# A gated mix of two linear-attention branches on one core: x and two weights loaded by transposing DMAs in place of plain loads, TensorE transposes and copies

## The chip, the core and the metric

The kernel runs on one core of a Trainium2 chip. The core has five engines with a queue of instructions each: TensorE (PE; its weight loads are listed apart as PEld), VectorE (DVE), ScalarE (ACT), GpSimd (POOL) and SyncE (SP), which here only issues DMAs. ScalarE can issue DMAs too. All of them share 16 DMA engines. The metric is the device time of one execution in microseconds (us). The median of three runs of the kernel before is 398.64 us (396.17 to 399.18).

## What is computed

S = 2048 tokens of D = 640 bf16 numbers, 32 heads of 20. Two branches read the same x, and a gate mixes them. The first branch (A) is linear attention with softmax feature maps, the second (B) works in four segments of 512 tokens with causal softmax attention and a running memory.

```python
def _A_ref(x, wqkv, w_phi, wo):
    q, k, v = split(x @ wqkv)                      # per head, 20 wide
    pq = einsum('bhsd,hdf->bhsf', q, w_phi); pk = einsum('bhsd,hdf->bhsf', k, w_phi)
    phi_q = concat([softmax(pq), softmax(-pq)]); phi_k = concat([softmax(pk), softmax(-pk)])
    kv = einsum('bhsf,bhsd->bhfd', phi_k, v); z = einsum('bhsf->bhf', phi_k)
    o = einsum('bhqf,bhfd->bhqd', phi_q, kv) / (einsum('bhqf,bhf->bhq', phi_q, z)[..., None] + 1e-06)
    return merge_heads(o) @ wo
...
x = A_x
g = sigmoid((x * gate_w).sum(-1, keepdims=True))
return g * _A_ref(x, A_wqkv, A_w_phi, A_wo) + (1 - g) * _B_ref(x, B_wq, B_wk, B_wv, B_wo, B_beta)
```

## The kernel before, in words

Everything that contracts over D needs x with D on the partitions. So `xT` is [128, 5, 2048]: five blocks of 128 features, 2048 tokens each. In the kernel before, x comes in as eight plain loads of two chunks of 128 tokens (`x_nat`, `emit_xload`, L98 to L101, through a pool of six buffers), and `emit_xT` (L186) turns one chunk: five TensorE transposes into a PSUM tile `xtp` (L189), then one ScalarE copy to `xT` (L191).

The key projection of branch A and the feature map `w_phi` are both linear, so they are folded into one weight: `WkA` = Wk times a block-diagonal `Wphi`. The product needs Wk transposed. `emit_foldT` (L168) does that block row by block row: five transposes of `wnat_k` (L171) and a copy to `WkT` (L173). `emit_foldM` (L175) then multiplies `WkT` with `Wphi` in six pieces (L179) and copies the result to `WkA` (L184). `Wphi` is made on VectorE from `Wc` (the loaded `w_phi`) and a mask (L160). The query weight takes the same way into `WqA`, with `wnat_q` and the same `WkT` buffer, inside and after the main loop. `WvA` holds the value weight in two halves of 320 columns, with the gate weight `gw5` as column 320 of each (L312), so that the gate's logit comes out beside the values.

The order of the first stage is written out by hand for all engines (`manual_schedule`, L90): each engine's queue follows the program text. That stage is:

1. Loads. ScalarE's queue issues three of five pieces of `wnat_k`, SP the rest: `Wc`, two pieces of `wnat_k`, two `x_nat`, `gw5`, two halves of `WvA`, four more `x_nat`, `beta_b`, two more `x_nat`.
2. 25 transposes of the identity as a warm-up of TensorE (L299), the transposes of `wnat_k`, the five folds to `WkA`, and with them the first four chunks of `xT`.
3. The main loop over 16 chunks (L317). Each pass transposes chunk sc + 4, and `emit_a1` (L207) makes `pk` and `pv`, ten products each (L213), with `xT` as the stationary operand. Its column choice is strided: pass sc takes every fourth token of segment sc // 4, so the first four passes need the first 512 tokens. ScalarE makes exp(pk) and exp(-pk) in `Ek` (L217) and copies `pv` to `vA` (L219); VectorE sums `Ek` per head (`ksum`, L221) and takes the reciprocal (`krec`, L224); GpSimd multiplies them into `EkSn` (L225). `Ek` has three buffers, the PSUM pool `aps` four.
4. `emit_zmove` (L230), once per pass: two DMAs on SP's queue that lay the chunk of `EkSn` into `Z`, 16 destination partitions each, eight rows of 640 per partition. After the third pass SP also issues `wnat_q` (L323); passes 9 to 13 transpose it.
5. The five folds to `WqA`, then `kv_ps` = EkSn^T vA (L373) for five blocks j in the order 0, 3, 1, 2, 4, masked into `kvn` (L378). Between the blocks VectorE adds up the 32 rows of `Z` (`emit_zadd`, L238); the first of these additions needs all 32 Z moves, since each move fills every fourth row.
6. `pq` and its exponentials `Eq` (L266, L271), and from there the rest of branch A (L488 on) and branch B (L570 on).

SP works through its queue in order. Each DMA takes one of eight completion counters in turn, and an issue waits until the DMA that held the counter before has landed; so an issue can be held by one some eight places ahead of it, and it always follows what is queued before it.

Of the kernel before, what the change touches and what calls it, by code (L numbers as in the profile page):

```python
# [9 lines left out]
BF16 = mybir.dt.bfloat16  # L10
# [5 lines left out]
def kernel(  # L16
# [15 lines left out]
    nc = tc.nc  # L32
    P = 128
    S = 2048
    D = 640
    H = 32
    DH = 20
    KC = D // P
    NCH = S // P
    NSEG = 4  # L40
    L = S // NSEG
# [3 lines left out]
    x2 = A_x[0]  # L45
# [5 lines left out]
    xT = const.tile([P, KC, S], BF16, name="xT")  # L51
    beta_b = const.tile([P, H], BF16, name="beta_b")
    ident_b = const.tile([P, P], BF16, name="ident_b")
# [16 lines left out]
    Aw = a_stack.enter_context(tc.tile_pool(name="Aw", bufs=1, side="right"))  # L70
    wq_stack = ExitStack()
    wq_hold = wq_stack.enter_context(tc.tile_pool(name="wq_hold", bufs=1))
    x_stack = ExitStack()
    xload = x_stack.enter_context(tc.tile_pool(name="xload", bufs=6))
    aps_stack = ExitStack()
    aps = aps_stack.enter_context(tc.tile_pool(name="aps", bufs=4, space=bass.MemoryType.PSUM))

    wnat_k = wq_hold.tile([P, KC, D], BF16, name="wnat_k", tag="wnat")
    Wc = wq_hold.tile([P, KC, DH], BF16, name="Wc")
    x_nat = []  # L80
    WkA = Aw.tile([P, KC, D], BF16, name="WkA")
    WqA = Aw.tile([P, KC, D], BF16, name="WqA")
    WvA = Aw.tile([P, KC, 2, 321], BF16, name="WvA")
    xv = x2.rearrange("(c p) d -> p c d", p=P)

    def wsrc(lo):
        return A_wqkv[:, lo:lo + D].rearrange("(c p) n -> p c n", p=P)
# [3 lines left out]
        engines={mybir.EngineType.PE, mybir.EngineType.Activation, mybir.EngineType.DVE,  # L91
                 mybir.EngineType.Pool, mybir.EngineType.SP}))
    gw5 = const.tile([KC, P], BF16, name="gw5")
    for c in (0, 2, 4):
        nc.scalar.dma_start(out=wnat_k[:, c], in_=wsrc(D)[:, c])
    nc.sync.dma_start(out=Wc, in_=A_w_phi.rearrange("h f g -> (h f) g").rearrange("(c p) g -> p c g", p=P))

    def emit_xload():  # L98
        x_nat.append(xload.tile([P, 2, D], BF16, name="x_nat"))
        c0 = 2 * len(x_nat) - 2  # L100
        nc.sync.dma_start(out=x_nat[-1], in_=xv[:, c0:c0 + 2, :])  # L101

    for c in (1, 3):
        nc.sync.dma_start(out=wnat_k[:, c], in_=wsrc(D)[:, c])
    for n in range(2):
        emit_xload()
    nc.sync.dma_start(out=gw5, in_=gate_w.rearrange("(c p) -> c p", p=P))
    for bk in range(2):
        nc.sync.dma_start(out=WvA[:, :, bk, 0:320], in_=wsrc(2 * D)[:, :, bk * 320:(bk + 1) * 320])
    for n in range(4):  # L110
        emit_xload()
    nc.sync.dma_start(out=beta_b, in_=B_beta.partition_broadcast(P))

    nc.gpsimd.memset(ident_b, 0.0)
    nc.gpsimd.affine_select(out=ident_b, in_=ident_b, pattern=[[-1, P]],
# [42 lines left out]
    def emit_Wphi(j):  # L158
        h0, h1 = TH[j]
        nc.vector.tensor_tensor(out=Wphi[:, j, 0:h1 - h0, :],  # L160
                                in0=Wc[:, j:j + 1, :].to_broadcast([P, h1 - h0, DH]),
                                in1=wmask[:, j, h0:h1, None].to_broadcast([P, h1 - h0, DH]),
                                op=ALU.mult)

    def w2tile(name):
        return aps.tile([P, 2, 512], F32, name=name, tag="w2")

    def emit_foldT(wn, WT, ic, eng):  # L168
        tp = aps.tile([P, KC, P], BF16, name="wtp", tag="w2")
        for cc in range(KC):  # L170
            nc.tensor.transpose(out=tp[:, cc, :], in_=wn[:, ic, cc * P:(cc + 1) * P],  # L171
                                identity=ident_b)
        eng(out=WT[:, :, ic * P:(ic + 1) * P], in_=tp)  # L173

    def emit_foldM(WT, dst, ic):  # L175
        ps = w2tile("fold_ps")
        for n, (j, bk, lo, hi) in enumerate(PIECES):
            h0 = TH[j][0]
            nc.tensor.matmul(ps[:, bk, (lo - 16 * bk) * DH:(hi - 16 * bk) * DH],  # L179
                             lhsT=WT[:, j, ic * P:(ic + 1) * P],  # L180
                             rhs=Wphi[:, j, lo - h0:hi - h0, :].rearrange("p h d -> p (h d)"),
                             start=(n in FIRST), stop=(n in LAST))
        eng = nc.vector.tensor_copy if ic % 2 == 0 else nc.scalar.copy
        eng(out=dst[:, ic, :].rearrange("p (b n) -> p b n", b=2), in_=ps[:, :, 0:320])  # L184

    def emit_xT(sc):  # L186
        tp = aps.tile([P, KC, P], BF16, name="xtp", tag="w2")
        for c in range(KC):
            nc.tensor.transpose(out=tp[:, c, :], in_=x_nat[sc // 2][:, sc % 2, c * P:(c + 1) * P],  # L189
                                identity=ident_b)  # L190
        nc.scalar.copy(out=xT[:, :, sc * P:(sc + 1) * P], in_=tp)  # L191

    WkT = wq_hold.tile([P, KC, D], BF16, name="WkT")

    kv_stack = ExitStack()
    a1w = kv_stack.enter_context(tc.tile_pool(name="a1work", bufs=3, side="right"))
# [10 lines left out]
    def emit_a1(sc):  # L207
        pk, pv = w2tile("pk"), w2tile("pv")
        for ps, W, n in ((pk, WkA, 320), (pv, WvA, 321)):
            for bk in range(2):  # L210
                for c in range(KC):
                    rhs = WvA[:, c, bk, :] if W is WvA else WkA[:, c, bk * 320:(bk + 1) * 320]
                    nc.tensor.matmul(ps[:, bk, 0:n], lhsT=xTk[:, c, sc // 4, sc % 4], rhs=rhs,  # L213
                                     start=(c == 0), stop=(c == KC - 1))
        Ek = a1w.tile([P, 2, D], BF16, name="Ek")
        for sgn in range(2):
            nc.scalar.activation(out=Ek[:, sgn, :].rearrange("p (b n) -> p b n", b=2),  # L217
                                 in_=pk[:, :, 0:320], func=ACT.Exp, scale=1.0 - 2.0 * sgn)
        nc.scalar.copy(out=vA[:, sc], in_=pv[:, :, 0:321])  # L219
        ksum = a1w.tile([P, 2 * H], F32, name="ksum")  # L220
        nc.vector.tensor_reduce(out=ksum, in_=Ek.rearrange("p s (h f) -> p (s h) f", f=DH),  # L221
                                axis=AX.X, op=ALU.add)
        krec = a1w.tile([P, 2 * H], F32, name="krec")
        nc.vector.reciprocal(out=krec, in_=ksum)  # L224
        nc.gpsimd.tensor_tensor(  # L225
            out=EkSn[:, sc].rearrange("p s (h f) -> p (s h) f", f=DH),
            in0=Ek.rearrange("p s (h f) -> p (s h) f", f=DH),
            in1=krec[:, :, None].to_broadcast([P, 2 * H, DH]), op=ALU.mult)

    def emit_zmove(sc):  # L230
        g, r = divmod(sc, 4)
        for sgn in range(2):
            nc.sync.dma_start(out=Z[64 * sgn + 16 * g:64 * sgn + 16 * g + 16, r:32:4],
                              in_=EkSn[:, sc, sgn, :])
# [62 lines left out]
    warm = aps.tile([P, KC, P], BF16, name="warm", tag="w2")  # L297
    for n in range(25):
        nc.tensor.transpose(out=warm[:, n % KC, :], in_=ident_b, identity=ident_b)  # L299
    for n in range(KC):  # L300
        emit_foldT(wnat_k, WkT, n, nc.vector.tensor_copy if n in (0, 2) else nc.scalar.copy)
        if n == 3:
            for j in range(KC):
                emit_Wphi(j)
    for n in range(KC):
        emit_foldM(WkT, WkA, n)
        if n in (1, 3):
            for sc in (n - 1, n):
                emit_xT(sc)
    gw_ps = aps.tile([P, KC], BF16, name="gw_ps", tag="w2")  # L310
    nc.tensor.transpose(out=gw_ps, in_=gw5, identity=ident_b[0:KC, 0:KC])
    nc.vector.tensor_copy(out=WvA[:, :, :, 320:321],  # L312
                          in_=gw_ps[:, :, None, None].to_broadcast([P, KC, 2, 1]))
    for n in range(2):
        emit_xload()
    wnat_q = wq_hold.tile([P, KC, D], BF16, name="wnat_q", tag="wnat")
    for sc in range(NCH):  # L317
        if sc + 4 < NCH:
            emit_xT(sc + 4)
        emit_a1(sc)  # L320
        emit_zmove(sc)
        if sc == 2:
            nc.sync.dma_start(out=wnat_q, in_=wsrc(0))  # L323
        if sc == 7:
            omgh_b, CM = emit_beta()
        if 9 <= sc < 14:
            emit_foldT(wnat_q, WkT, sc - 9, nc.scalar.copy if sc % 2 else nc.vector.tensor_copy)
    x_stack.close()
    for n in range(KC):
        emit_foldM(WkT, WqA, n)  # L330
    wq_stack.close()
    resW = ctx.enter_context(tc.tile_pool(name="resW", bufs=1))
    WqB = resW.tile([P, KC, H, 32], BF16, name="WqB")
# [6 lines left out]
        out=xg, in0=vA[:, :, 0, 320].rearrange("p (g u) -> p u g", u=4)[:, :, :, None].to_broadcast([P, 4, 4, 4]),  # L340
# [229 lines left out]
    with ExitStack() as bctx:  # L570
# [231 lines left out]
        for k in range(NG):  # L802
            s, g = divmod(k, G)
# [91 lines left out]
        tp = bps.tile([P, 4, P], BF16, name="otp4", tag="ps1")  # L895
# [47 lines left out]
```

## Time and profile before

| | |
|---|---|
| profiled execution, its own time | 397.7 us |
| its span, first to last instruction | 395.9 us |
| median of the three runs | 398.64 us |
| PE busy | 350.4 us (89%), 3620 instructions |
| DVE / ACT / POOL busy | 294.9 / 290.2 / 180.0 us |
| mean granted TensorE clock | 0.984 |
| first `pk` / first `pv` / end of the last `pv` | 13.06 / 14.41 / 61.05 us in the chain |
| transposes into `xtp` / `wtp` | 80 / 50 of 219 ns each (they overlap: a group of five holds TensorE 0.28 us) |
| copies L191 / L173 on ACT | 16 of 698 ns / 6 of 697 ns (median) |
| Z moves: first issue, last issue, last landing | 20.40, 66.53, 70.71 us |

How to read it: the page of the profile gives the busy time of each engine, the span in slices, the chain of work that ended last (followed back from the last instruction, at each step to what released it), the costliest groups of instructions, and the DMA issues. A line number is that of the kernel. Busy time is an average over stages with different limits; what a change in one stage is worth is read from the wait that ends last there. TensorE's products are pipelined, so the ends of single ones overlap.

### The profile page before, as it was taken

What the parts mean: (1) busy time and instruction counts of PE and PEld (TensorE: products, weight loads), DVE (VectorE), ACT (ScalarE), POOL (GpSimd) and SP (SyncE); (2) the same over time, 40 slices, a digit from 0 to 9 for tenths busy, and PEclk for the clock granted to TensorE, in tenths of its full rate; (3) what the DMA queues carried; (4) which work ended last, traced back from release to release, by engine and by line L of the source; (5) the groups of instructions that cost most, each with busy time, mean ns of one, the idle gap of its engine ahead of it and who ended that gap; (6) DMA issues with size and microseconds to landing.
All of it is one profiled execution on the core that took longest, in us unless ns stands there. A gap on an engine that the chain in (4) does not pass through costs nothing.

```text
span 395.9 us, 8984 instructions
## 1 busy us (share of the span) xinstructions
PE 350.4 (89%) x3620; PEld 226.0 (57%) x3653; DVE 294.9 (74%) x622; ACT 290.2 (73%) x398; POOL 180.0 (45%) x260
## 2 busy tenths in 40 slices
PE   7899999998689996989999898889899897888894
PEld 6688888744467774634454455455555554444452
DVE  3466976887867861858667798998887888788854
ACT  5788873187746675468888998887978786789840
POOL 8177697000467872014554535445453534343420
PEclk9999999999989999999999999999999999999968
DMA  8659699900000000200000000000000000000002
GB/s 235 200 105 174 88 126 125 303 35 2 0 2 2 2 2 0 84 0 2 2 0 2 2 19 2 17 19 2 18 18 17 2 18 20 17 2 19 17 18 66
DMA packets 16851, 17.64 MB, mean 45 GB/s; under 512 B 1962, under 2 KB 16810, under 8 KB 16810
## 3 DMA queue, kind: packets, MB, share of 16 engines
q1 hardware_dynamic: 15946, 16.26, 19.5%
q10 hardware_dynamic: 864, 0.82, 0.7%
q8 instruction: 28, 0.46, 0.5%
q14 instruction: 13, 0.11, 0.1%
HBM read 9.21 MB, written 2.62 MB: 30 GB/s over the span
## 4 chain that ended last, share of the span: by engine, by line
PE 53%; DVE 16%; ACT 15%; issue 6%; DMA 5%; POOL 3%; SPq 0%; ACTq 0%; DVEq 0%; POOLq 0%
ACT PT L655 12%; PE qT_ps L612 8%; PE st_ps L651 7%; PE proj L589 6%; PE oA_ps L475 5%; PE pk L213 4%; PE o_ps L738 4%; PE pv L213 4%; PE pq L266 3%; DMA Z<-EkSn 3%; DVE tt L460 2%; DVE qT L616 2%; PE num L416 2%; DMA x_nat<-in_A_x_dram 2%; DVE ndsb L676 2%
## 5 line engine op out<-in xcount | busy, mean ns | idle before, releaser
L655 ACT ACTIVATE PT<-st_ps 128x1024 bf16<-128x1024 f32 (+1 forms) x144 | 155.8, 1120 | 29.1 <-PE st_ps L651 23.6
L660 POOL TENSOR_SCALAR_AFFINE_SELECT PT<-PT 128x512 bf16<-128x512 bf16 x128 | 82.6, 662 | 94.2 <-ACT PT L655 94.1
L651 PE MATMUL st_ps<-qT,kT 32*128 32x384 bf16 (+3 forms) x512 | 51.3, 301 | 9.3 <-ACT PT L655 7.0
L225 POOL TENSOR_TENSOR EkSn<-Ek,krec 128x1280 bf16<-128x1280 bf16 x16 | 37.6, 2359 | 18.4 <-DVE krec L224 17.3
L612 PE MATMUL qT_ps<-xT,WqB 128*128 128x512 bf16 x130 | 37.6, 381 | 2.1 <-issue 0.8
L213 PEld LDWEIGHTS <-xT 128*128 128x128 bf16 x320 | 35.4, 113 | 6.7
L651 PEld LDWEIGHTS <-kT 32*128 32x128 bf16 x512 | 17.3, 91 | 37.4 <-issue 30.1
L589 PEld LDWEIGHTS <-xT 128*128 128x128 bf16 x320 | 28.0, 98 | 14.4 <-issue 3.1
L616 DVE CAST qT<-qT_ps 128x512 bf16<-128x512 f32 x32 | 22.1, 690 | 17.8 <-PE qT_ps L612 17.8
L221 DVE TENSOR_REDUCE ksum<-Ek 128x64 f32<-128x1280 bf16 x16 | 23.7, 1478 | 13.0 <-ACT Ek L217 12.9
L460 DVE TENSOR_TENSOR tt<-num,rr 128x640 f32<-128x640 f32 x32 | 24.6, 813 | 10.8 <-PE num L416 6.0
L545 POOL TENSOR_TENSOR oA<-tt 128x640 bf16<-128x640 f32 x16 | 24.7, 1545 | 12.4 <-DVE tt L460 6.5
L271 ACT ACTIVATE Eq<-pq 128x1024 bf16<-128x1024 f32 x20 | 19.4, 1021 | 12.6 <-DMA WkB<-in_B_wk_dram 7.2
L475 PE MATMUL oA_ps<-WoA,oTA 128*128 128x320 bf16 x160 | 25.8, 310 | 2.6 <-ACT oTA L468 2.5
L477 ACT CAST outA<-oA_ps 128x320 bf16<-128x320 f32 x32 | 13.6, 426 | 19.4 <-PE oA_ps L475 19.4
L589 PE MATMUL proj<-WvB,xT 128*128 128x320 bf16 x160 | 26.6, 300 | 0.5 <-ACT ek L603 0.5
L589 PE MATMUL proj<-WkB,xT 128*128 128x320 bf16 x160 | 26.5, 300 | 0.5 <-ACT outA L477 0.5
L676 DVE CAST ndsb<-nd_ps 128x512 bf16<-128x512 f32 x32 | 22.0, 686 | 5.8 <-PE nd_ps L670 5.6
L217 ACT ACTIVATE Ek<-pk 128x640 bf16<-128x640 f32 x32 | 20.8, 701 | 7.4 <-PE pk L213 5.0
L703 POOL TENSOR_TENSOR Msb<-Msb,mtmp 128x84 f32<-128x84 f32 x24 | 8.7, 361 | 38.6 <-DVE mtmp L700 38.6
L738 PE MATMUL o_ps<-WoB,oT 128*128 128x320 bf16 x120 | 21.6, 313 | 3.9 <-DVE mtmp L700 3.9
L416 PEld LDWEIGHTS <-Eq 128*128 128x128 bf16 x384 | 18.7, 97 | 11.0 <-issue 7.9
(150 smaller groups left out, 690.5 us busy)
## 6 DMA issues: line engine op xcount, KB each, us to landing
Z<-EkSn SPq DMA_DIRECT2D x32, 160.0 KB, 4.9
x_nat<-in_A_x_dram SPq DMA_DIRECT2D x8, 320.0 KB, 6.8
out_dram<-outA SPq DMA_DIRECT2D x13, 160.0 KB, 1.8
WvA<-in_A_wqkv_dram SPq DMA_DIRECT2D x2, 400.0 KB, 7.0
wnat_q<-in_A_wqkv_dram SPq DMA_DIRECT2D x1, 800.0 KB
WkA<-in_B_wq_dram SPq DMA_DIRECT2D x1, 800.0 KB, 6.4
WvA<-in_B_wv_dram SPq DMA_DIRECT2D x2, 400.0 KB, 8.9
WkB<-in_B_wk_dram SPq DMA_DIRECT2D x1, 800.0 KB, 10.6
```

What stands on the lines that cost most here:

```text
L213: nc.tensor.matmul(ps[:, bk, 0:n], lhsT=xTk[:, c, sc // 4, sc % 4], rhs=rhs, start=(c == 0), stop=(c == KC - 1))
L225: nc.gpsimd.tensor_tensor(out=EkSn[:, sc].rearrange("p s (h f) -> p (s h) f", f=DH), in0=Ek.rearrange("p s (h f) -> p (s h) f", f=DH), in1 ...
L460: nc.vector.tensor_tensor(out=tt[:, sgn].rearrange("p (b h) d -> p b h d", b=2), in0=ps, in1=csb, op=ALU.mult)
L475: nc.tensor.matmul(o_ps, lhsT=oT[:, k5, :], rhs=WoA[:, k5, half * 320:(half + 1) * 320], start=(k5 == 0), stop=(k5 == KC - 1))
L589: nc.tensor.matmul(ps, lhsT=xT[:, cc, sc * P:(sc + 1) * P], rhs=W[:, cc, half * 320:(half + 1) * 320], start=(cc == 0), stop=(cc == KC - 1))
L612: nc.tensor.matmul(qT_ps, lhsT=WqB[:, cc, 4 * g:4 * g + 4, :], rhs=xT[:, cc, s * L:(s + 1) * L], start=(cc == 0), stop=(cc == KC - 1))
L616: nc.vector.tensor_copy(out=qT, in_=qT_ps)
L651: nc.tensor.matmul(st_ps[:, i - i0, o:o + L - c * P], lhsT=kT[32 * i:32 * i + 32, c * P:(c + 1) * P], rhs=qT[32 * i:32 * i + 32, c * P:L], ...
L655: nc.scalar.activation(out=PT[:, i0:i0 + nh], in_=st_ps[:, :, 0:PT.shape[-1]], func=ACT.Exp, scale=SCALE_B)
L660: nc.gpsimd.affine_select(out=PT[:, :, o:o + P], in_=PT[:, :, o:o + P], pattern=[[0, 4], [1, P]], compare_op=ALU.is_ge, fill=0.0, base=0, ...
L676: nc.vector.tensor_copy(out=ndsb, in_=nd_ps)
L738: nc.tensor.matmul(o_ps, lhsT=oT[:, k5, :], rhs=WoB[:, k5, hs], start=(k5 == 0), stop=(k5 == KC - 1))
```

## The change

x, the key weight and the query weight of branch A are now read from DRAM by DMAs that transpose on the way, straight into `xT`, `WkT` and a new `WqT`. `emit_foldT`, `emit_xT`, `emit_xload`, the pool of `x_nat` and both `wnat` buffers are gone. The small loads `Wc`, `gw5` and `beta_b` go to ScalarE's queue; all transposing loads and `WvA` are on SP's, at its head, with `WqT` last and the Z moves behind them. `emit_foldM` for the queries reads `WqT`. The order of everything else is kept.

```diff
-    x_stack = ExitStack()
-    xload = x_stack.enter_context(tc.tile_pool(name="xload", bufs=6))
...
-    wnat_k = wq_hold.tile([P, KC, D], BF16, name="wnat_k", tag="wnat")
+    WkT = wq_hold.tile([P, KC, D], BF16, name="WkT")
+    WqT = wq_hold.tile([P, KC, D], BF16, name="WqT")
...
-    for c in (0, 2, 4):
-        nc.scalar.dma_start(out=wnat_k[:, c], in_=wsrc(D)[:, c])
-    nc.sync.dma_start(out=Wc, in_=A_w_phi.rearrange("h f g -> (h f) g").rearrange("(c p) g -> p c g", p=P))
-
-    def emit_xload():
-        x_nat.append(xload.tile([P, 2, D], BF16, name="x_nat"))
-        c0 = 2 * len(x_nat) - 2
-        nc.sync.dma_start(out=x_nat[-1], in_=xv[:, c0:c0 + 2, :])
-
-    for c in (1, 3):
-        nc.sync.dma_start(out=wnat_k[:, c], in_=wsrc(D)[:, c])
-    for n in range(2):
-        emit_xload()
-    nc.sync.dma_start(out=gw5, in_=gate_w.rearrange("(c p) -> c p", p=P))
+    nc.scalar.dma_start(out=Wc, in_=A_w_phi.rearrange("h f g -> (h f) g").rearrange("(c p) g -> p c g", p=P))
+    nc.scalar.dma_start(out=gw5, in_=gate_w.rearrange("(c p) -> c p", p=P))
+    nc.scalar.dma_start(out=beta_b, in_=B_beta.partition_broadcast(P))
+
+    def load_T(dst, src):
+        nc.sync.dma_start(out=dst, in_=src, transpose=True)
+
+    for c in range(KC):
+        load_T(WkT[:, :, c * P:(c + 1) * P], A_wqkv[c * P:(c + 1) * P, D:2 * D])
+    for c in range(4):
+        load_T(xT[:, :, c * P:(c + 1) * P], x2[c * P:(c + 1) * P, :])
     for bk in range(2):
         nc.sync.dma_start(out=WvA[:, :, bk, 0:320], in_=wsrc(2 * D)[:, :, bk * 320:(bk + 1) * 320])
-    for n in range(4):
-        emit_xload()
-    nc.sync.dma_start(out=beta_b, in_=B_beta.partition_broadcast(P))
+    for g in range(1, 4):
+        load_T(xT[:, :, g * L:(g + 1) * L], x2[g * L:(g + 1) * L, :])
+    load_T(WqT, A_wqkv[:, 0:D])
...
-    for n in range(KC):
-        emit_foldT(wnat_k, WkT, n, nc.vector.tensor_copy if n in (0, 2) else nc.scalar.copy)
-        if n == 3:
-            for j in range(KC):
-                emit_Wphi(j)
+    for j in range(KC):
+        emit_Wphi(j)
     for n in range(KC):
         emit_foldM(WkT, WkA, n)
-        if n in (1, 3):
-            for sc in (n - 1, n):
-                emit_xT(sc)
...
-    for n in range(2):
-        emit_xload()
-    wnat_q = wq_hold.tile([P, KC, D], BF16, name="wnat_q", tag="wnat")
     for sc in range(NCH):
-        if sc + 4 < NCH:
-            emit_xT(sc + 4)
         emit_a1(sc)
         emit_zmove(sc)
-        if sc == 2:
-            nc.sync.dma_start(out=wnat_q, in_=wsrc(0))
         if sc == 7:
             omgh_b, CM = emit_beta()
-        if 9 <= sc < 14:
-            emit_foldT(wnat_q, WkT, sc - 9, nc.scalar.copy if sc % 2 else nc.vector.tensor_copy)
-    x_stack.close()
     for n in range(KC):
-        emit_foldM(WkT, WqA, n)
+        emit_foldM(WqT, WqA, n)
```

More of the change, by code (lines that the diff above doesn't have):

```diff
@@ L72 @@
     wq_hold = wq_stack.enter_context(tc.tile_pool(name="wq_hold", bufs=1))
-    x_stack = ExitStack()
-    xload = x_stack.enter_context(tc.tile_pool(name="xload", bufs=6))
     aps_stack = ExitStack()
     aps = aps_stack.enter_context(tc.tile_pool(name="aps", bufs=4, space=bass.MemoryType.PSUM))
-    wnat_k = wq_hold.tile([P, KC, D], BF16, name="wnat_k", tag="wnat")
+    WkT = wq_hold.tile([P, KC, D], BF16, name="WkT")
+    WqT = wq_hold.tile([P, KC, D], BF16, name="WqT")
     Wc = wq_hold.tile([P, KC, DH], BF16, name="Wc")
-    x_nat = []
     WkA = Aw.tile([P, KC, D], BF16, name="WkA")
@@ L83 @@
     WvA = Aw.tile([P, KC, 2, 321], BF16, name="WvA")
-    xv = x2.rearrange("(c p) d -> p c d", p=P)
     def wsrc(lo):
@@ L166, in w2tile @@
         return aps.tile([P, 2, 512], F32, name=name, tag="w2")
[L168 to L173, printed above, removed]
     def emit_foldM(WT, dst, ic):
@@ L184, in emit_foldM @@
         eng(out=dst[:, ic, :].rearrange("p (b n) -> p b n", b=2), in_=ps[:, :, 0:320])
[L186 to L193, printed above, removed]
     kv_stack = ExitStack()
```

## The prediction

> **What bounds the kernel now.** The change touches only the first stage, up to about 76 us, so I read that stage and ask what ends it. First the chain of waits in order of time (start, length, what). Three places of it:
>
> ```profile
> 4.79 7.77 DMA x_nat<-in_A_x_dram
> 12.56 0.05 issue
> 12.60 0.45 PE xtp L189 x5
> 13.06 1.36 PE pk L213 x10
> 14.41 1.37 PE pv L213 x10
> 15.79 0.28 PE xtp L189 x5
> ...
> 65.94 0.55 SPq L233
> 66.49 0.04 issue
> 66.53 4.18 DMA Z<-EkSn
> 70.71 0.03 issue
> 70.75 0.49 DVE Z L238
> ```
>
> The loop over the 16 chunks starts when a load of x has landed (12.56), then runs at TensorE's pace: 0.28 transposes + 1.36 + 1.37 = 3.01 us a chunk. The stage ends not on TensorE but on the move of `EkSn` into `Z`: the last of its 32 DMAs lands at 70.71, and the first addition of line 238 starts 0.04 us later. Behind that addition VectorE has `kvn` (L378) queued, and behind `kvn` TensorE has the last `kv_ps` products and all of `pq`; the waits show them released in that order at 73.25 and 73.62. So a microsecond later at 70.71 is a microsecond at the end. (The chain also names a Z move ahead of the `EkSn` at 63.59; there `krec` had ended only at 63.41, as 0.14 us before every other `EkSn`, so I read that step as the loop's own pace.)
>
> Second, the stretches (start:end, length, busy PE, PEld, DVE, ACT, POOL, clock, DMA share, GB/s):
>
> ```profile
> 10.00:12.00 2.00, 0.99 (x13) 0.74 (x11) 1.04 (x3) 1.94 (x4) 0.00 (x0) 1.00 1.08 359
> ...
> 35.00:38.00 3.00, 3.00 (x27) 2.53 (x26) 2.03 (x3) 2.58 (x6) 2.35 (x2) 1.00 1.16 120
> 56.00:59.00 3.00, 3.00 (x25) 2.50 (x22) 2.03 (x3) 2.58 (x5) 2.35 (x2) 1.00 1.16 125
> 65.00:68.00 3.00, 2.73 (x44) 2.55 (x42) 1.51 (x4) 0.00 (x0) 2.55 (x2) 1.00 0.97 124
> ```
>
> The reader is to see that a DMA share of about 1 means 359 GB/s for plain loads at 10:12, but only 120 to 125 GB/s where nothing but Z moves is in flight. A chunk's two moves are 327.7 KB, so at 124 GB/s they need 2.64 us of all DMA engines; 16 chunks need 42.2 us. Z is nearly a second bound beside TensorE, and it can't catch up.
>
> Third, the DMA issues (size, median us from issue to landing), for prices:
>
> ```profile
> wnat_k<-in_A_wqkv_dram SPq DMA_DIRECT2D x2, 160.0 KB, 4.0
> out_dram<-outA SPq DMA_DIRECT2D x2, 80.0 KB, 1.6
> Wc<-in_A_w_phi_dram SPq DMA_DIRECT2D x1, 25.0 KB, 2.7
> ```
>
> **What it removes.** 130 TensorE transposes and 26 copies. Inside the loop, all on TensorE's path: twelve `xtp` and five `wtp` groups of 0.28 us, 4.8 us, of which one `xtp` lies ahead of the first `pv`. The copies (0.7 us of ScalarE or 0.45 of VectorE each) lie beside TensorE and are worth nothing alone: without them ScalarE needs 1.30 + 0.69 = 2.0 us a chunk, VectorE 2.0 and GpSimd 2.36, all under 2.73. That 2.73 is seen: the last two chunks have no transposes left and `pk` starts at 55.59 and 58.32. Counted from the first `pv`, the loop takes 61.05 - 14.41 = 46.6 us now and 1.37 + 15 x 2.73 = 42.3 then: -4.3 us.
>
> **What it adds and moves.** 13 transposing loads on SP's queue: five of 164 KB (`WkT`), four of 164 KB (`xT`), then the two plain `WvA` loads, three of 655 KB and one of 819 KB: 4.26 MB, or 26 units of 164 KB. Issuing costs what plain ones do, 0.47 us each. `Wc`, `gw5` and `beta_b` go to ScalarE's queue ahead of its table load; 3 x 0.45 us there is no more than the three `wnat_k` issues they replace (1.39 us). `Wphi` waits for `Wc` (landing near 3.5) and takes 1.38 us, so it is ready near 5, before the second `WkT` piece: hidden. What matters is that every one of these loads is issued ahead of the first Z move. In the built program SP's order is all 13 transposing loads, then Z; and each SP issue waits for the landing of one about eight before it, so the third and fourth chunk's moves wait on the late `xT` and `WqT` loads by name. Queued behind SP there is only Z (and the second branch's weights, first read at 102.69, with room). Who waits for Z is told above. Today SP has Z's first move out at 20.40 and the 0.82 MB of `wnat_q` after the third chunk.
>
> **The unknown price p of one 164 KB unit.** No row of this trace transposes in a DMA. From below: as a plain load, 164 KB at 359 GB/s, 0.46 us. From above: if a unit is written as 5,120 pieces of 32 bytes, priced as below, 8.8 us. The nearest row is `Wc`: 128 x 5 rows of 40 bytes, 640 pieces, landed in 2.7 us where a plain 80 KB needs 1.6; so 640 pieces cost 1.1 us. A unit cut into 128 x 5 runs of 128 elements is also 640 pieces. If piece cost and data overlap p is 1.1, if they add it is 1.1 + 0.46 = 1.56; I take 1.3, an estimate (126 GB/s).
>
> [...]
>
> **The sum at p = 1.3.**
> - `xT`'s fourth piece lands at 0.8 + 9 x 1.3 + 1.6 = 14.1 (0.8 is SP's first issue, 1.6 the landing of a small transfer). The folds of `WkT` are done before it: its fifth piece lands at 8.9, and 1.3 us of products and copy follow.
> - `WvA` (0.82 MB, 2.3 us) lands at 16.4, its gate column 0.2 later, and the first `pv` starts at 16.7 against 14.41: +2.3. Loop end 16.7 + 42.3 = 59.0 against 61.05: -2.0. The other `xT` loads are early: the first 655 KB lands at 21.6, its chunk comes at 26.
> - All loads in front of Z leave the DMA engines at 0.8 + 26 x 1.3 + 2.3 = 36.9. Five chunks of `EkSn` are waiting by then. Z needs 42.2 us and 1.6 to land: 80.7 against 70.71: +10.0.
>
> The later of the two decides: the stage ends 10.0 us later although the loop ends 2.0 earlier. The profiled execution is 397.7 us around its span of 395.9, 0.9 under the median 398.64: 397.7 + 10.0 = 407.7, and 408 against that median. From 76 us on the instruction order of every engine is the same, so the shift passes on unchanged. TensorE would then idle some 10 us before the last `kv_ps`; the granted clock is 1.00 in every stretch of this stage, which has no such gap, so a slower restart has no price from a row (bounds: nothing, or half speed over the 2 us of `kv_ps` that follow, 2 us more). [...]
>
> Because Z ends at 0.8 + 26p + 2.3 + 43.8, the break-even is p = 0.92 (179 GB/s): one per cent slower from p = 1.07, one per cent faster below 0.76 (215 GB/s).
>
> **The rivals.**
> - *Transposing loads run near plain speed* (p up to 0.76). Then Z starts with its first chunk and TensorE's pace decides. At p = 0.46 `WvA` lands at 8.8, the folds end near 8.2, the first `pv` starts at 9.7, the loop ends at 52.0: -9.0, 389. At p = 0.7 Z ends at 65.1: -5.6, 392. For it: 356 to 359 GB/s of plain loads and the -4.3 us that is certain once data is there. Against: the `Wc` row. 30%.
> - *The gain and the late Z cancel* (p from 0.76 to 1.07): 394 to 402. 15%.
> - *The forecast: Z starts late* (p from 1.07 to 2.0): 402 to 426, likeliest 408. For it: the share near 1 at 124 GB/s, which leaves no room to catch up. Against: if Z moves and transposes use different resources, they could overlap, and 42.2 us is too much. 40%.
> - *The transposing loads themselves starve the loop* (p over 2): at p = 3 the first `pv` starts at 32 and Z ends at 125, +54, 452; at 8.8 over 600. For it: 32-byte writes would be the shortest pieces in the program. Against: the loads are issued as tiles of 16 x 128, a form made for it. 15%. That the loads do not transpose at all but are cut up element by element would land here too.
>
> **The numbers.** About one per cent, 4 us, is what a measurement can tell. Faster by more: 30%. Within: 15%. Slower: 40 + 15 = 55%. The range goes from 389 (fast end) to 426 (p = 2.0); it leaves out nearly only the starving case.
>
> **What would show it.** Right: the first Z move's data late (well after 30 us), DMA share near 1 from 1 us to the end of the stage, the chain running through Z moves without `pk`/`pv` between them, the first addition of L238 near 81, `pk` every 2.73 us from about 14. Wrong: `pk` before 10 and Z's last landing near 62 (fast), or waits of TensorE on `xT` loads inside the loop (starved). The step that everything hangs on is p; the next is that Z can't run beside the transposes.

## The result, and the profile after

The changed kernel takes 414.15 us (median of 4 runs, 413.36 to 416.17) against 397.66 us (4 runs) for the kernel before, measured with it: ratio 1.042, 95% interval [1.036, 1.048]. It is slower. The profiled execution took 416.17 us around a span of 414.5; its own shift against the profiled execution of before is 416.17 - 397.7 = +18.5 us, two more than that of the medians (+16.5). The three other runs have spans of 411.6 to 412.9, so times read from this one trace stand a little high.

The same places as before, now of the kernel after. First SP's timeline (start, length from first to last issue, line, what):

```profile
0.81 6.62 SPq L96 DMA_TRANSPOSE WkT<-in_A_wqkv_dram  x5
7.47 5.24 SPq L96 DMA_TRANSPOSE xT<-in_A_x_dram  x4
12.75 1.15 SPq L103 DMA_DIRECT2D WvA<-in_A_wqkv_dram  x2
13.95 11.45 SPq L96 DMA_TRANSPOSE xT<-in_A_x_dram  x3
25.44 3.76 SPq L96 DMA_TRANSPOSE WqT<-in_A_wqkv_dram  x1
36.63 44.14 SPq L211 DMA_DIRECT2D Z<-EkSn  x32
```

One piece of 164 KB keeps SP busy for 1.28 us, where the plain `wnat_k` issue of the same size kept it for 0.5. All loads are issued by 29.2; yet the first Z move goes out only at 36.63. It waits for no load: there is no `EkSn` to move. TensorE's timeline says why (last column: idle time ahead, and what ended it):

```profile
14.60 0.43 PE L191 MATMUL pk<-WkA,xT 128*128 128x320 bf16 x1 [3.48 <-DMA xT<-in_A_x_dram]
28.07 2.59 PE L191 MATMUL pk<-WkA,xT 128*128 128x320 bf16 x9 [13.04 <-DMA xT<-in_A_x_dram]
30.45 2.89 PE L191 MATMUL pv<-WvA,xT 128*128 128x321 bf16 x10
```

The first product of `pk` runs when the fourth piece of `xT` is there. The other nine start 13 us later, again behind an `xT` load, though pass 0 reads nothing but the first 512 tokens, which had landed when the first product ran. In the chain of waits (start, length, what):

```profile
18.65 3.44 SPq L96
22.09 0.04 issue
22.14 5.88 DMA xT<-in_A_x_dram
28.02 0.05 issue
28.07 2.59 PE pk L191 x9
30.65 2.68 PE pv L191 x10
33.34 1.48 PE pk L191 x10
34.81 1.37 PE pv L191 x10
...
79.58 0.55 SPq L211
80.13 0.04 issue
80.17 7.99 DMA Z<-EkSn
88.19 0.05 DVEq L216
88.24 0.04 issue
88.28 0.50 DVE Z L216
```

The load that ends the wait is the third of the late ones, tokens 1536 to 2047. The first `pk` and `pv` then take 2.59 and 2.68 us, nearly twice the 1.36 and 1.37 of the later ones. The last Z landing is at 88.16, against 70.71 before, and the next addition of line 216 (L238 in the kernel before) follows at 88.28. The last group of `kv_ps` and the stretches around it (start:end, length, busy PE, PEld, DVE, ACT, POOL, clock, DMA share, GB/s):

```profile
90.12 3.89 PE L335 MATMUL kv_ps<-vA,EkSn 128*128 128x140 bf16 x32 [3.97 <-DVE kvn L340]
```

```profile
60.00:70.00 10.00, 10.00 (x75) 8.29 (x74) 9.12 (x11) 7.13 (x12) 9.03 (x4) 1.00 0.59 85
70.00:76.00 6.00, 6.00 (x58) 5.12 (x56) 4.90 (x5) 4.68 (x7) 6.00 (x4) 1.00 1.12 121
88.00:92.00 4.00, 1.88 (x17) 1.88 (x17) 3.54 (x9) 0.00 (x0) 0.00 (x0) 0.51 1.12 318
```

Z moves still cost a DMA share over 1 at 121 GB/s (70:76); at 60:70 the share is only 0.59, because no `EkSn` is ready (SP waits for one before each of the 16 pairs, 30.5 us in all). At 88:92 the granted clock is 0.51, after a gap of 3.97 us, and the 32 products that took 2.14 us before take 3.89. The issue of `WqT` (us to landing, so it had landed near 31.2):

```profile
WqT<-in_A_wqkv_dram SPq DMA_TRANSPOSE x1, 5.8
```

VectorE's timeline around the five additions, first of the kernel before, then of the kernel after:

```profile
70.53 0.30 DVE L378 TENSOR_TENSOR kvn<-kv_ps,wmw 128x140 bf16<-128x140 f32 x1 [0.67 <-PE kv_ps L373]
```

```profile
83.93 0.48 DVE L216 TENSOR_TENSOR Z<-Z 128x640 bf16<-128x640 bf16 x1
86.04 0.49 DVE L216 TENSOR_TENSOR Z<-Z 128x640 bf16<-128x640 bf16 x1 [1.63 <-DMA Z<-EkSn]
88.28 1.54 DVE L216 TENSOR_TENSOR Z<-Z 128x640 bf16<-128x640 bf16 x3 [1.75 <-DMA Z<-EkSn]
```

So the first addition does not need all 32 moves, as was said ahead of the prediction: it adds row 1 to row 0, which the passes up to 13 have filled; the second needs pass 14, and only the third needs the last pass. In the kernel before the first addition came at 70.75 behind the `kvn` of 70.53, and the third, the first that needed the landing at 70.71, at 71.79: Z had 1.1 us in hand there.

**Where the time went.** `pq` starts at 94.01 against 75.77: +18.2. Followed back: the last `EkSn` is ready at 79.57 against 65.92 (+13.65); from there to the last Z landing it is 8.6 us against 4.8 (+3.8); two of the five additions are already done by then, and so those 1.1 us are used up (-1.0); `kv_ps` runs at half clock (+1.75). Of the +13.65, 13.2 are the loop's end (74.24 against 61.05): the nine `pk` products start 15.0 us after the first `pk` of before, the two groups at half speed cost 1.2 + 1.3, and the loop gives 4.3 back.

### The profile page after: what moved, and what is told of

Its sections match the earlier page's. It is cut to its first block, busy times and chain, and to the rows that moved or that the text cites. A ratio compares the mean times of both kernels' runs of the same rounds, so it can differ in the third digit from the quotient of the medians.

```text
span 414.5 us, 8697 instructions
## 1 busy us (share of the span) xinstructions
PE 349.8 (84%) x3490; PEld 222.1 (54%) x3523; DVE 293.6 (71%) x618; ACT 276.7 (67%) x376; POOL 179.7 (43%) x260
## 4 chain that ended last, share of the span: by engine, by line
PE 47%; DVE 17%; ACT 14%; issue 7%; POOL 5%; SPq 5%; DMA 3%; DVEq 0%; POOLq 0%; ACTq 0%
ACT PT L617 12%; PE qT_ps L574 7%; PE st_ps L613 6%; PE proj L551 6%; PE oA_ps L437 5%; SPq L96 5%; PE o_ps L700 4%; PE pq L244 3%; POOL EkSn L203 3%; PE pk L191 3%; PE pv L191 3%; DVE tt L422 2%; DVE qT L578 2%; PE num L378 2%; DMA Z<-EkSn 2%
## 5 line engine op out<-in xcount | busy, mean ns | idle before, releaser
L191 PEld LDWEIGHTS <-xT 128*128 128x128 bf16 x320 | 36.9, 116 | 26.1 <-DMA xT<-in_A_x_dram 13.4
L191 PE MATMUL pk<-WkA,xT 128*128 128x320 bf16 x160 | 26.0, 311 | 16.5 <-DMA xT<-in_A_x_dram 16.5
L551 PEld LDWEIGHTS <-xT 128*128 128x128 bf16 x320 | 28.0, 98 | 14.4 <-issue 3.1
L249 ACT ACTIVATE Eq<-pq 128x1024 bf16<-128x1024 f32 x20 | 19.4, 1021 | 18.2 <-PE pq L244 17.9
L191 PE MATMUL pv<-WvA,xT 128*128 128x321 bf16 x160 | 25.9, 311 | 0.0
```

The costliest lines, as they stand in the source:

```text
L551: nc.tensor.matmul(ps, lhsT=xT[:, cc, sc * P:(sc + 1) * P], rhs=W[:, cc, half * 320:(half + 1) * 320], start=(cc == 0), stop=(cc == KC - 1))
```

## The experiments

My theory: the order of the loads and Z's need of DMA time were as predicted, but two things were not in its sum: a false wait of `pk` in pass 0 on the later parts of the `xT` tile, and half speed after TensorE's gaps. The first can be read in the built program: the second weight load of pass 0 (feature block 1) carries waits for all three later `xT` loads. It reads every fourth column of block 1; those loads write blocks 0 to 4 of other columns in the same tile, so the address ranges interleave though no byte is shared. The rival: late data (the loads, or Z behind them) explains all of it, and splitting the tile gains little.

### The tile cut in four

```diff
-    xT = const.tile([P, KC, S], BF16, name="xT")
+    xTg = [const.tile([P, KC, L], BF16, name=f"xT{n}") for n in range(NSEG)]
...
-        load_T(xT[:, :, g * L:(g + 1) * L], x2[g * L:(g + 1) * L, :])
+        load_T(xTg[g], x2[g * L:(g + 1) * L, :])
```

Every load, order and size is that of after; only the tile that holds x is four tiles.

> One tile of 128 x 5 x 2048 for x is replaced by four tiles of 128 x 5 x 512, one per segment; nothing else differs from the changed kernel. Theory A (the first weight load of the second feature block waits for all three later x loads, though it reads none of their bytes): that wait of 13.4 us is gone, the first pk starts at 14.6, the first pv at 18.8 when WvA has landed, the loop ends near 62 and the last Z move lands at 73 (Z starts when SP has issued its loads, 29.3, plus 42.2 and 1.6): about 400 us, ratio to before 1.006. Theory B (my prediction's: the loads' DMA work and Z behind it set the end, the wait of TensorE is only beside it): Z ends no earlier than 81 and the time stays at 408 or more, ratio 1.025.

404.38 us, ratio 1.018 [1.011, 1.025]. TensorE's and SP's timelines of it:

```profile
14.88 2.79 PE L191 MATMUL pk<-WkA,xT 128*128 128x320 bf16 x10 [3.98 <-DMA xT<-in_A_x_dram]
18.94 1.53 PE L191 MATMUL pv<-WvA,xT 128*128 128x321 bf16 x10 [1.27 <-DVE WvA L284]
```

```profile
26.53 3.93 SPq L96 DMA_TRANSPOSE WqT<-in_A_wqkv_dram  x1
30.58 38.00 SPq L211 DMA_DIRECT2D Z<-EkSn  x32
```

All ten `pk` products run at 14.9 and nothing in the loop waits for `xT` again: the false wait is shown, and is worth about 10 us (414.15 to 404.38, ratio 1.042 to 1.018). What is left is the case that the prediction described: Z moves stand behind the loads (first at 30.58, right behind `WqT`), and then take every DMA engine:

```profile
30.00:40.00 10.00, 10.00 (x76) 8.30 (x74) 7.24 (x9) 7.66 (x12) 8.38 (x5) 1.00 1.14 154
40.00:50.00 10.00, 10.00 (x75) 8.31 (x74) 9.55 (x14) 6.42 (x11) 5.92 (x3) 1.00 1.14 116
50.00:60.00 10.00, 10.00 (x75) 8.31 (x74) 8.98 (x9) 7.65 (x12) 10.00 (x6) 1.00 1.16 119
```

With a share of 1.14 to 1.16 at 116 to 154 GB/s, TensorE is busy all the time, yet Z's last landing is at 78.3, between the two expected (73 and 81), as the time is (400 and 408), and 7.6 us later than before. From the first issue to the last landing Z takes 47.7 us for its 5.24 MB, which is 110 GB/s.

### What the transposing loads cost: plain loads beside them, and fewer, larger ones

Three variants of the split kernel: `WvA` on ScalarE's queue from the start; `WvA` there and `WkT` and the first 512 tokens as one load each; and the same large loads with `WvA` behind them on SP.

```diff
+    for bk in range(2):
+        nc.scalar.dma_start(out=WvA[:, :, bk, 0:320], in_=wsrc(2 * D)[:, :, bk * 320:(bk + 1) * 320])
...
-    for c in range(KC):
-        load_T(WkT[:, :, c * P:(c + 1) * P], A_wqkv[c * P:(c + 1) * P, D:2 * D])
-    for c in range(4):
-        load_T(xTg[0][:, :, c * P:(c + 1) * P], x2[c * P:(c + 1) * P, :])
+    load_T(WkT, A_wqkv[:, D:2 * D])
+    load_T(xTg[0], x2[0:L, :])
```

> As e1_split, and the two WvA loads are issued from ScalarE's queue at the start. If the issues on SP (1.28 us each) hold up what is behind them, the first pv moves from 18.8 to 16.0, and SP is through with its loads at 28 in place of 29.3; Z then ends at 72: 399 us, ratio 1.003. If the DMA engines are the limit and not the issuing, the nine transposing loads land later by what WvA takes (2.3 us) and nothing is gained: 400 to 401 us.

> As e2_split_wv, and WkT and the first x segment come by one load each in place of five and four. If an issue costs 0.66 us plus 0.62 for each 164 KB (from 1.28 for one piece, 3.4 for four and 3.76 for five), SP has issued both by 8.0 in place of 12.7 and all its loads by 22; the first pv starts near 12.5, the loop ends at 55, Z lands at 66: 393 us, ratio 0.988. If the price is in the data and not in the issue, nothing moves: 399 us as e2_split_wv.

> e4_split_big_wv with WvA back on SP's queue, behind the WkT and first x loads. In e4_split_big_wv the single WkT load landed 8.86 us after its issue, beside WvA. If that was the DMA engines shared with WvA, WkT now lands near 6.5 and the first pk starts near 11 to 12, while WvA lands near 14 and holds the first pv there; if a large transposing load is slow by itself, WkT lands near 9.5 again and pk starts near 14. Time 401 either way, since Z is behind the loads in both.

| kernel | us, ratio to before | `WvA` | first `pv` | first Z move | last Z landing |
|---|---|---|---|---|---|
| e1_split | 404.38, 1.018 [1.011, 1.025] | SP | 18.94 | 30.58 | 78.3 |
| e2_split_wv | 404.07, 1.013 [1.005, 1.022] | ScalarE | 17.58 | 26.71 | 75.2 |
| e4_split_big_wv | 401.33, 1.010 [1.002, 1.018] | ScalarE | 15.67 | 23.83 | 70.6 |
| e3_split_big | 399.93, 1.006 [1.003, 1.009] | SP | 13.78 | 25.92 | 73.7 |

With 0.8 MB of `WvA` beside them (e2) the nine small transposing loads land no later: `pk` of pass 0 starts at 14.75, against 14.88 in e1. So they are not limited by DMA bandwidth there but by SP's issue, 1.28 us each (in after the DMA share at 8:12 is 0.77, at 124 GB/s). The large load shows the other regime. SP's first issue in e3 (4.02 us in e4), and what the first fold (L164) waits for, in e3 and then in e4:

```profile
0.81 3.69 SPq L96 DMA_TRANSPOSE WkT<-in_A_wqkv_dram  x1
...
7.26 3.88 PE L164 MATMUL fold_ps<-Wphi,WkT 128*128 128x240 bf16 x30 [2.98 <-DMA WkT<-in_A_wqkv_dram]
```

```profile
9.71 4.01 PE L164 MATMUL fold_ps<-Wphi,WkT 128*128 128x240 bf16 x30 [5.43 <-DMA WkT<-in_A_wqkv_dram]
```

One issue of 819 KB takes 3.69 us, five of 164 KB take 6.62. From 1.28 and 3.69 I estimate some 0.68 us per issue and 0.60 per 164 KB, so that even one endless issue would come to no more than 164 KB / 0.60 us = 273 GB/s. And the large load does suffer from `WvA` beside it: it lands at 9.7 in e4, at 7.2 in e3. That is most of why e4 missed its expectation for the first `pv` (12.5); the folds, which run at half speed (4.01 us for 30, at a granted clock of 0.50 at 10:14; the later ones of z_after take 1.61 for 24), come on top. The times expected of e2 (399, or 400 to 401) and e4 (393, or 399) were both missed upwards; that fewer, larger issues bring Z forward held (23.83 against 26.71), and e3 came out near its 401.

In bandwidth, by SP's issue times, the transposing loads come to 128 GB/s at 164 KB an issue (after) and to 222 GB/s at 819 KB (819 KB / 3.69 us, e3). Where they fill the DMA engines (28:30 of after, a share of 1.27) they reach 270 GB/s, against 359 GB/s for the plain loads of before at a share of 1.08 (10:12).

### The plain start kept, the late tokens transposed

`h1_plain_start` keeps the plain start of before (key weight and first 512 tokens through TensorE) and loads only the three later segments by transposing DMAs into tiles of their own; `wnat_q` stays plain.

```diff
-    for n in range(4):
-        emit_xload()
+    for g in range(1, 4):
+        nc.sync.dma_start(out=xTg[g], in_=x2[g * L:(g + 1) * L, :], transpose=True)
...
-        if sc + 4 < NCH:
-            emit_xT(sc + 4)
```

> The kernel before, with its plain loads and TensorE transposes for the key and query weights and the first 512 tokens, and transposing loads (one each, own tile each) only for the other three x segments, which are not needed before 24 us. The loop loses 12 groups of transposes of 0.28 us = 3.4 us and does not wait for the fifth chunk any more; the first pk starts near 12, Z still starts near 20 since SP has issued its loads by 17. Theory: loop end near 57.5, last Z landing 66.5: 393.5 us, ratio 0.989. Rival: the transposing loads crowd the DMA engines and Z comes late all the same: 398 or more.

395.79 us, ratio 0.996 [0.992, 1.000]. The loads no longer delay the start (`pk` of pass 0 at 11.86, first Z move at 19.38), the loop ends some 2.8 us earlier (58.2) and the last `kv_ps` starts at 70.90 against 73.62. The 393.5 expected was missed: the last landing is at 68.9, not 66.5, and of the 2.7 us at `kv_ps` 1.2 arrive at the end. The transposing DMA in itself is thus no loss; its place at the head of the stage is.

### Z's share of the DMA engines

A move writes 16 neighbouring partitions. The edit writes 16 that are 4 apart, with the same bytes; the 64 partitions of one sign are then summed in another order.

```diff
-            nc.sync.dma_start(out=Z[64 * sgn + 16 * g:64 * sgn + 16 * g + 16, r:32:4],
+            nc.sync.dma_start(out=Z[64 * sgn + g:64 * sgn + 64:4, r:32:4],
```

> The changed kernel, and each Z move writes 16 partitions that lie 4 apart (64 sgn + g + 4 i) in place of 16 neighbours (64 sgn + 16 g + i); bytes, rows and their number are the same, the per-feature sum is taken in another order. Theory: the Z moves are slow (120 to 125 GB/s at a DMA share of 1) because of where they write. A pair then takes about 1.3 us in place of 2.6, the last landing follows the last EkSn (79.6) by 3.5 us, 83 in place of 88.2, and TensorE has no long gap ahead of the last kv_ps: 407 us, ratio to before 1.022. Rival: the limit is the 1,280-byte row or the read side; then Z stays at 120 GB/s, the last landing at 88 and the time at 414.

> The kernel before with the same edit of the Z moves and nothing else. There Z was not late by itself: only the last pair's own time shrinks (4.8 us from its issue to landing becomes about 3.5). Theory: last landing 69.3 in place of 70.7, 396 us, ratio 0.996. Rival: no change, 397.

> e4_split_big_wv (own tiles, large transposing loads, WvA from ScalarE's queue) with the same edit of the Z moves. If Z is what ate its earlier loop end, Z now lands 3.5 us after the last EkSn (about 62.5), 66 in place of 70.7, and kv_ps runs without the gap (2.1 in place of 3.7 us): about 394 to 395 us, ratio 0.992. Rival (Z's rate does not depend on where it writes): 401, ratio 1.01.

> h1_plain_start with the same edit of the Z moves. Last EkSn at 62.9, last landing 66.4 in place of 69.0: 393 us, ratio 0.989. Rival: 396, ratio 0.996, as h1_plain_start. A third case: the stage ends earlier and the rest of the kernel gives it back, as h1_plain_start did with 2.7 us less at the last kv_ps but 1.2 at the end; then 394 to 395.

| kernel with this edit | us | ratio to before |
|---|---|---|
| of after (z_after) | 415.10 | 1.042 [1.035, 1.048] |
| of before (z_before) | 397.68 | 1.002 [0.999, 1.006] |
| of e4 (z_e4) | 396.34 | 0.994 [0.990, 0.998] |
| of h1 (z_h1) | 395.40 | 0.996 [0.992, 1.001] |

z_before came out as its rival: Z had 1.1 us in hand, so there was no wait to take away (the last `kv_ps` waits 0.66 us for `kvn`, 0.67 in before). z_h1 came out between its third case (394 to 395) and its rival (396). z_e4 has a ratio 0.016 below that of e4, yet stays a little above the 394 to 395 expected. Stretches, same columns as above, of after, then of z_after, and the last `kv_ps` of z_after:

```profile
40.00:50.00 10.00, 10.00 (x76) 8.30 (x74) 7.18 (x9) 7.41 (x12) 8.39 (x5) 1.00 0.54 98
```

```profile
40.00:50.00 10.00, 10.00 (x75) 8.29 (x74) 7.21 (x8) 7.73 (x12) 8.39 (x5) 1.00 0.37 104
70.00:76.00 6.00, 5.92 (x58) 5.01 (x57) 4.86 (x7) 5.04 (x8) 6.00 (x3) 1.00 0.56 154
...
348.00:364.00 16.00, 13.10 (x77) 5.27 (x79) 8.53 (x19) 8.43 (x12) 4.36 (x7) 0.57 0.03 11
```

```profile
86.19 2.14 PE L335 MATMUL kv_ps<-vA,EkSn 128*128 128x140 bf16 x32 [0.66 <-DVE kvn L340]
```

In the same stretches the spread moves take a smaller share of the engines: 0.37 for 0.54 at 40:50, and 0.56 for 1.12 at 70:76 while moving more (154 GB/s against 121). Nothing waits for Z any more: the last `kv_ps` starts at 86.19 and at full speed, and `pq` 5.7 us earlier than in after. That shows that the last 5 to 6 us of the stage's shift were Z's backlog and its gap. But my 407 us for z_after missed: the end did not move. In the profiled execution the gain is there until late: the last `proj` of the values starts at 341.8 against 347.5 in after. The last `qT_ps` starts at 387.3 against 387.9, so 5.1 of the 5.7 us are lost between the two. There the granted clock is 0.57 (348:364), where after has 1.00: a stretch of half clock far behind the stage took the gain.

Moves of neighbours ran at 110 GB/s over the whole backlog of e1_split, and at 116 to 125 in single stretches, with the share above 1. The runs show what the choice of partitions does to the share, not by what mechanism; that a pair takes half its time, 1.3 us in place of 2.6, was my estimate.

### Dummy transposes in TensorE's two gaps

`w_after` is after with 230 dummy transposes ahead of the first `pk` and 55 ahead of the last `kv_ps`.

```diff
+    def fill(n_tr):
+        ft = aps.tile([P, KC, P], BF16, name="warm2", tag="w2")
+        for n in range(n_tr):
+            nc.tensor.transpose(out=ft[:, n % KC, :], in_=ident_b, identity=ident_b)
+
+    fill(230)
...
+        if j == 4:
+            fill(55)
```

> The changed kernel with dummy TensorE transposes of the identity where TensorE waits: 230 between gw_ps and the first pk (some 15 us, within the wait that ends at 28.07), 55 ahead of the last kv_ps block (3 us, within the wait that ends at 90.1). Theory (TensorE restarts at half speed after a long wait): the first pk and pv take 1.4 us each in place of 2.6 and 2.7, the last kv_ps 2.14 in place of 3.89 and the first pq products 0.22 each, with no granted clock of 0.5 near 90; the start of the loop does not move. Then 409 to 411 us, ratio 1.031. Rival (the first products are slow because of what the loads do to memory, and kv_ps because of the Z traffic): durations as before, 414.

TensorE's timeline, first a line of after, then of w_after:

```profile
8.80 0.95 PE L166 MATMUL fold_ps<-Wphi,WkT 128*128 128x240 bf16 x6 [1.17 <-DMA WkT<-in_A_wqkv_dram]
```

```profile
7.83 0.57 PE L166 MATMUL fold_ps<-Wphi,WkT 128*128 128x240 bf16 x6 [0.31 <-DMA WkT<-in_A_wqkv_dram]
...
23.22 0.30 PE L191 MATMUL pk<-WkA,xT 128*128 128x320 bf16 x1
28.86 2.59 PE L191 MATMUL pk<-WkA,xT 128*128 128x320 bf16 x9 [5.34 <-DMA xT<-in_A_x_dram]
...
85.73 3.23 PE L289 MATMUL warm<-ident_b 128*128 128x128 bf16 x55
89.35 0.53 PE L341 MATMUL kv_ps<-vA,EkSn 128*128 128x140 bf16 x6 [0.38 <-DVE kvn L346]
91.23 1.77 PE L341 MATMUL kv_ps<-vA,EkSn 128*128 128x140 bf16 x26 [1.35 <-issue]
```

Ahead of `kv_ps` the fill worked: 0.53 + 1.77 us of products, full speed, clock 1.00 at 88:92, beside the same DMA share of 1.12 as in after, so the Z traffic is not the cause. But TensorE stood for 1.35 us between the two groups, for a reason that the trace doesn't name, and `pq` came only 1.0 us earlier than in after. Ahead of `pk` the fill ended too early, a gap of 5.34 us was left, and the nine products took 2.59 again, though folds and fill had run at full speed ahead of it. The granted clock of w_after reads 1.00 at 26:28 and 0.50 at 30:32: the speed halved behind that gap. In after, however, TensorE was at half speed already before its gap of 13 us: six folds took 0.95 us, against 0.57 in w_after behind the same loads. z_after, the same program up to the Z moves, has a granted clock of 0.50 in its records from 8 us on, through the whole gap.

The time missed its expectation, 414.83 us, 1.045 [1.041, 1.049], because little was gained: the nine `pk` start at 28.86 against 28.07 and are no faster, and 1.0 us is left at `pq`. The span of the profiled execution is 1.3 us shorter than that of after (413.2 against 414.5), too little for the medians to tell.

The gaps with half speed behind them are 3.97 us in after and 5.34 us in w_after; in e4 `kv_ps` took 3.74 us already after a gap of 2.80.

### A version that beats both

`z_h2` is z_h1 with `WqT` by a transposing DMA at the third pass in place of `wnat_q` and its 25 transposes. `z_h2_fill` adds 32 dummy products in the 1.8 us in which TensorE waits ahead of `den`.

```diff
-            nc.sync.dma_start(out=wnat_q, in_=wsrc(0))
+            nc.sync.dma_start(out=WqT, in_=A_wqkv[:, 0:D], transpose=True)
...
-        if 9 <= sc < 14:
-            emit_foldT(wnat_q, WkT, sc - 9, nc.scalar.copy if sc % 2 else nc.vector.tensor_copy)
```

```diff
+                for n in range(32):
+                    nc.tensor.matmul(dt2[:, 0:P], lhsT=ident_b, rhs=ident_b, start=True, stop=True)
```

> z_h1 with the query weight also by a transposing load, issued on SP after the third chunk's Z moves in place of wnat_q; five wtp groups (1.4 us of TensorE) and their copies go, and with them TensorE's wait on VectorE in 42 to 47 us. SP is held 3.9 us by the issue, so the fourth chunk's Z moves start that much later; with the spread Z writes (a share near 0.5) they catch up. Loop end 56 in place of 58.3, the first pq near 71 in place of 73.1: 393 us, ratio 0.990. Rival: Z comes late again or the loop is bound by GpSimd's 2.36 us and the wait moves there: 395.4 as z_h1.

> z_h2 with 32 dummy products of 128x128 (about 57 ns each, 1.8 us) on TensorE ahead of the first `den`, in the 1.80 us in which it waits there for `kvd` (90.8 to 92.6 of z_h2); their results are overwritten. Nothing is left out. Theory (the gap there brings on the half clock of 94 to 97, which gives 1.7 us of the gain back): the ten `pq` products after `den` take 2.3 instead of 3.99, the granted clock is 1.00 from 92 to 98, `num` starts 1.5 us earlier than 99.81, and the time is 393.5, ratio 0.990. Rival (the half clock comes from work done over a longer time, not from that gap): 3.99 or near it again, 395.3, ratio 0.995. Second rival: the clock holds there but a later stretch takes it, as in w_after: 395.3 too, with the 100 to 112 or 372 to 382 stretch longer.

z_h2 takes 395.29 us, ratio 0.995 [0.992, 0.998]; z_h2_fill 393.37 us, 0.990 [0.986, 0.994]. In z_h2 the stage ends 4.7 us before that of before (`pq` at 71.07). TensorE's timelines around `den`, first of z_h2, then of z_h2_fill:

```profile
92.58 1.36 PE L410 MATMUL den<-kvd,Eq 128*128 128x24 bf16 x48 [1.80 <-DVE kvd L253]
93.79 3.99 PE L266 MATMUL pq<-xT,WqA 128*128 128x512 bf16 x10
```

```profile
90.13 1.95 PE L493 MATMUL den<-ident_b 128*128 128x128 bf16 x32
92.11 1.34 PE L410 MATMUL den<-kvd,Eq 128*128 128x24 bf16 x48
93.31 2.32 PE L266 MATMUL pq<-xT,WqA 128*128 128x512 bf16 x10
```

The fill gives the 1.7 us back as expected (2.32 in place of 3.99), and the time went down by the 1.9 us expected; the intervals of the two overlap, so that difference is likely rather than shown. z_h2 itself missed its 393, though `pq` came at 71 as forecast: the 3.99 us are part of that. The gap alone is not the whole cause: the traces of the other kernels have the same wait of 1.8 us there, and `pq` took 2.32 behind it in six (before, e1, e2, z_before, z_h1, w_after), where the granted clock stays at 1.00, and 3.6 to 4.0 in four (e3, e4, h1, z_e4), where it falls to 0.50 to 0.53 (100:102 in e4, 96:98 in z_e4).

## Why the prediction was right, and where it was wrong

The direction and the range held (408, 389 to 426, measured 414.15), and the likeliest case, a late Z, was a true part of it. But that the number is so near is in part luck: of the 18.2 us at `pq`, 13.2 came through a loop that the sum had ending 2.0 us earlier. With the false wait gone, e1_split is 7.4 us behind its kernel before (404.38 against 397.01), where the sum has 10.0.

- **The price p.** 1.28 us was measured for a 164 KB piece against 1.3 taken, by luck: the reason given (640 pieces in the DMA engines) fell, it is SP's issue. "Issuing costs what plain ones do, 0.47 us each" was wrong, and so p is not one price: 0.86 a unit at 655 KB (3.44 / 4, from one of three that took 3.3 to 4.7), 0.75 at 819 KB (3.76 / 5). All loads were issued by 29.2 and `WqT` had landed near 31, not at 36.9.
- **The wait at 70.71.** "So a microsecond later at 70.71 is a microsecond at the end" was a misreading: the addition at 70.75 did not need that landing, and the first 1.1 us cost nothing. z_before shows the same.
- **The start.** The fourth piece was put at 14.1, and 14.6 was measured; the first `pv` at 16.7, and 30.65 was measured. The step that failed is "The other `xT` loads are early: the first 655 KB lands at 21.6, its chunk comes at 26". It asked when a chunk's own tokens come, not what the program makes pass 0 wait for. All three loads were waited for in pass 0, to 28.07. The case of waits on `xT` loads had been given 15%, but at a price p over 2; it came at p = 1.28, by the tile. In e1_split, without that wait, the first `pv` is at 18.94: `WvA` lands 2 us later than the sum had it.
- **The loop.** -4.3 us was right: from the first `pv` it takes 74.24 - 30.65 = 43.6, of which 1.3 is the half speed of that `pv`.
- **Z.** That Z starts late behind the loads and can't catch up at a share above 1 was right, shown by e1_split. Its landing there, 78.3 against 80.7 predicted, hides two misses: Z started at 30.58, not at 36.9, and took 47.7 us, not 42.2 + 1.6, at 110 GB/s over the whole and not at the 124 of one short stretch (from 69.5 on the weights of branch B load beside it). In after, Z was first starved of `EkSn`, so its last landing was 88.16.
- **"The later of the two decides"** held, but the loop ended 13.2 us later, not 2.0 earlier; the backlog of Z added 3.8 behind it.
- **The restart.** Its bounds were nothing or 2 us: 1.75 at `kv_ps`, and half speed at the loop's start, 2.5 us, had not been foreseen; TensorE was in it since the folds.
- **"The shift passes on unchanged"** held between the two profiled executions (+18.2 at `pq`, +18.5 at the end), and the 1.3 us of w_after arrived too, but it is no rule: z_after moved the stage by 5.7 us and the end by nothing.

What stays open: what decides in which later stretch the clock is halved. The kernels' traces have it at other places (0.63 at 128:132 in after, 0.57 at 120:132 in w_after and at 348:364 in z_after). One minus the mean granted clock, times the span, comes to 6 to 26 us; not all of that lies on the path (16 x 0.43 = 6.9 us at 348:364 of z_after cost 5.1). So a gain of a few microseconds in the first stage can't be read off the end alone.

## What to carry to other kernels

A load that fills part of a tile can hold readers of another part (13.0 us of waiting in after, some 10 us of the time): where a strided read and a later load interleave in one tile, give each load its own tile, and read the waits of the first reader in the built program before you price the load. Put transposing loads where the issuing queue is idle and the data is not yet wanted, in few and large issues (3.69 us of SP for one of 819 KB, 6.62 for five of 164 KB), and keep them out of the way of moves that need the DMA engines for the whole stage (a share of 1.14 to 1.16 in e1_split). And follow a gain to the end by the clock as well as by the instructions.

## What the runs showed of the hardware

- A transposing load holds SP's queue for 1.28 us at 164 KB (after) and 3.7 to 4.0 us at 819 KB (3.69 in e3, 3.76 in after, 4.02 in e4; 4.83 beside Z moves, in z_h2); a plain one of 164 KB for 0.5 (before).
- Moves of the same bytes to 16 partitions took a DMA share of 0.37 at 104 GB/s and 0.56 at 154 when these lie 4 apart (z_after), and of 0.54 at 98 and 1.12 at 121 in the same stretches when they are neighbours (after).
- After gaps of 2.80, 3.97 and 5.34 us TensorE's next products took nearly twice their time (`kv_ps` 3.74 after 2.80 in e4 and 3.89 after 3.97 in after, for 2.14 in before; nine `pk` 2.59 after 5.34 in w_after, where ten take 1.36 in before). After 1.8 us they did so in some kernels (`pq` 3.99 in z_h2) and not in others (2.32 in before).
- In after the view shows a clock of 1.00 in the first 30 us although folds (six in 0.95 us, 0.57 in w_after), first `pk` (2.59) and first `pv` (2.68, later ones 1.37) took nearly twice as long; its records begin only at 33.4 us, where the speed is full. The granted clock in the records does not show every such stretch.
